# The first two blocks of a gated feed-forward layer walk the same weight chunks one step apart

## The chip, the cores and the metric

One core of a Trainium2 chip. The metric is the device time of one launch in microseconds (us). The kernel before takes 1696.36 us (median of 3 runs, 1696.3 to 1697.64).

## The reference

Pooled attention, then two feed-forward layers, all in float32:

```python
# attention: batch 8, heads 8, S 576, D 64; keys and values are means over 8 rows, 72 are left
scores = scale * q @ k_p.T; attn = softmax(scores); x = attn @ v_p     # x: 4608 tokens x 512
# layer 1 (512 -> 2048 -> 512)
h = x @ w_in
g = where(h >= 1, h, where(h <= -1, 0, (h + 1)**2 / 4))
x = g @ w_out
# layer 2 (512 -> 2048 -> 512)
out = (max(x @ w_in2, 0)**2) @ w_out2
```

The weights arrive as 64-bit floats, so that the kernel itself converts them to 32 bits.

## The kernel before

**Tiles.** 4608 tokens are 36 tiles of 128 for the attention, and 9 blocks of 512 (four tiles each) for layer 1. The 2048 hidden columns are cut in 16 chunks of 128 (`KF`). Every float32 product is made of three products in a reduced format: an operand `a` is split into `hi` (a rounded copy, written by ScalarE) and `lo` (`a - hi`, by VectorE), and `hi*hi + hi*lo + lo*hi` is summed. So a *first product* of one block and one chunk (`gemm1`, L613) is 12 matmuls of 512 columns into one bank, and a *second product* (`gemm2`, L672) is 12 into the four accumulator banks of its block.

**Steps.** The main loop (L852) goes through 144 steps of layer 1, block after block, chunk after chunk, and then 16 of layer 2's first block. Step s issues the first product of s and the second product of step s - 2 (`LAG`). `step_ops` (L627) issues what VectorE and ScalarE do for it: two activations and one VectorE instruction that make `g` from the bank (L643 to L653), `gh` and `gl`, its split (L654, L660), the split of the next weight chunks (`split_hi`, `split_lo`, L211 to L219), and, at a block's last chunk, the copy of the accumulators to DRAM (`evac_acc`).

**Weights of layer 1.** Each of the 32 chunks (16 of `w_in`, 16 of `w_out`) is loaded as 512 KB and converted once (`convert_w`, L136): two ScalarE instructions (its "head"), three VectorE instructions and one on GpSimd (its "tail"). The result stays in SBUF for all nine blocks. Its split into `hi` and `lo` does not stay: every block makes it again, for both weights. In the first block the `lo` of `w_in` is made by GpSimd from chunk 2 on (L602), later by VectorE. Conversions run through the opening and the steps of block 0.

**Attention.** It is cut in units: `k` (keys of a batch), `q` (transpose of a tile's queries), `s` (scores, half a tile each), `x` (times the values). The string `before` (L479) lists what runs ahead of the steps: keys and values of batch 0, tiles 0 to 3 (block 0), and five conversion heads. There the normalized weights are transposed by TensorE (`p` units, L422). Later tiles write them to DRAM (`do_stores`), fetch them back (`fetch`) and transpose with VectorE (`turn`, L447). The table `slots` gives each unit of the later tiles a half step: tiles 4 to 7 (block 1) lie in steps 2 to 14, those of block 2 from step 12 on.

**Who sets the order.** The order written in the program is a priority. The framework plans each engine's queue from it ahead of the run with its own table of costs, taking the first instruction whose inputs it believes to be ready; on the chip each queue then runs strictly in that order, and waits where the belief was wrong. All DMAs are issued from one queue, SP's.

Of the kernel before, what the change touches and what calls it, by code (L numbers as in the profile page):

```python
# [20 lines left out]
LAG = 2  # L21
LEAD = 8
# [9 lines left out]
def pooled_attention_moe_moe(  # L32
# [11 lines left out]
    nc = tc.nc  # L44
# [27 lines left out]
    gp = left.enter_context(tc.tile_pool(name="gp", bufs=LAG + 2))  # L72
# [9 lines left out]
    x2t = dr.tile([DM, NT], F32, name="x2t")  # L82

# [120 lines left out]
    def stream_w2(kind, f):  # L204

        t = wq.tile([P, 2, 2, HB], F32R, tag="w", name="wt")
        n = 2 * (f // NG)
        nc.sync.dma_start(out=t.bitcast(F32), in_=w2c[kind][f % NG][:, n:n + 2])
        return None, t[:, :, 0, :], t[:, :, 1, :]

    def split_hi(kind, m, f):  # L211
        src = w_sb[kind, m, f]
        hi = ws.tile(w_shape(kind), F32R, tag=f"w{kind}hi", name=f"w{kind}hi")
        lo = ws.tile(w_shape(kind), F32R, tag=f"w{kind}lo", name=f"w{kind}lo")
        nc.scalar.activation(out=hi, in_=src, func=AF.Copy)  # L215
        return src, hi, lo

    def split_lo(eng, src, hi, lo):
        eng.tensor_tensor(out=lo, in0=src, in1=hi.bitcast(F32), op=ALU.subtract)  # L219
# [122 lines left out]
    def unit_s(t, g):  # L342
# [8 lines left out]
        if g == 0:  # L351
            pn_t[t] = (
                early_pn(t) if t in (0, 1, 3) else at.tile([P, H, SP], F32, tag="pn", name="pn", bufs=1),
                at.tile([P, H, 1], F32, tag="mx", name="mx"),
            )
            if t in ON_ACT:
                sums[t] = at.tile([P, H, 1], F32, tag="sm", name="sm", bufs=3)
# [33 lines left out]
    def early_pn(t):  # L391
        flat = pad[t % 3].rearrange("p n h c -> p (n h c)")
        return flat[:, 0:H * SP].rearrange("p (h s) -> p h s", h=H)

    def norm(t):
        pn, mx = pn_t[t] if t < TB0 else pn_t.pop(t)
# [8 lines left out]
        if t < TB0:  # L405
            nc.vector.tensor_tensor(out=pn, in0=pn, in1=sm.to_broadcast([P, H, SP]), op=ALU.mult)
            return
# [43 lines left out]
    def unit_x(t):  # L451
# [30 lines left out]
        " lo hi1 lo head head"  # L482
    ).split()
    slots, pool_at = {}, {}
    for t in range(TB0, NTILE):

        if t < 2 * TB0:
            c = (2, 5, 8, 10)[t - TB0]
            at_s0, at_s1, at_q, at_x = 2 * c, 2 * c + 1, 2 * c + 2, (15, 19, 25, 29)[t - TB0]
        else:  # L490
            c = KF - 4 + 4 * (t - 2 * TB0)
            at_s0, at_s1, at_q, at_x = 2 * c, 2 * c + 2, 2 * c + 4, 2 * c + 11
        todo = {at_s0: ("s", t, 0), at_s1: ("s", t, 1), at_x: ("x", t)}
        if t + 1 < NTILE:
            todo[at_q] = ("q", t + 1)
        if t in first_tile:
            b = first_tile.index(t)
            todo.update({2 * c - 2 + i // 2: ("k", b, i) for i in (0, 2)})
            for i in range(2 * NP):
                at_p = 2 * (c + i - 8) + (i >= NP) * 8 if b > 1 else (0, 1, 2, 3, 6, 8, 10, 12)[i]  # L500
                pool_at[at_p] = 2 * NP * b + i + 1
        assert not slots.keys() & todo.keys()
        slots.update(todo)

        assert 2 * KF * (t // TB0 - 2) <= at_x - 2 < at_x + 2 < 2 * KF * (t // TB0), t
# [46 lines left out]

    def do_later():
        for f in later:
            f()
        later.clear()
# [12 lines left out]
    def do_norms():  # L569
        for t in norms:  # L570
            norm(t)
        stores.extend(norms)
        norms.clear()
# [10 lines left out]
    steps = [(0, j, f) for j in range(NB) for f in range(KF)] + [(1, 0, f) for f in range(KF)]  # L584
    NS, NS0 = len(steps), NB * KF
    split = {}
    n_split = {"i": 0, "o": 0}
    x2_t, g_t, acc = {}, {}, {}

    def next_hi(kind, n):  # L590
        s = n_split[kind]
        if s >= min(n, NS):
            return
        m, _, f = steps[s]
        split[kind, s] = split_hi(kind, m, f) if m == 0 else stream_w2(kind, f)
        n_split[kind] += 1
        return s

    def next_lo(kind, s):
        if s is None or steps[s][0] == 1:  # L600
            return
        split_lo(nc.gpsimd if kind == "i" and 2 <= s < KF else nc.vector, *split[kind, s])  # L602
# [10 lines left out]
    def gemm1(s):  # L613
        m, j, f = steps[s]
        _, wh, wl = split.pop(("i", s))
        xh, xl = x_t[j] if m == 0 else x2_t[j]
        ph = ps_h.tile([P, TB], F32, tag="h", name="ph")
        i = 0
        for kk in range(KD):
            for a, c in ((wh, xh), (wh, xl), (wl, xh)):  # L620
                if m == 1:
                    a = a.rearrange("p o (k c) -> p o k c", k=2)[:, kk // 2]
                nc.tensor.matmul(out=ph, lhsT=a[:, kk % a.shape[1], :], rhs=c[:, kk, :], start=(i == 0), stop=(i == 3 * KD - 1))  # L623
                i += 1
        return ph

    def step_ops(s, ph, evac_a, evac_b, fill):  # L627


        m, j, f = steps[min(s, NS - 1)]  # L630
        do_later()
        do_fetches()
        next_lo("o", next_hi("o", s - LAG + 2))
        if ph is not None:
            gh = gp.tile([P, TB], F32R, tag="gh", name="gh")
            gl = gp.tile([P, TB], F32R, tag="gl", name="gl")
            g = ap.tile([P, TB], F32, tag="g", name="g", bufs=1)
            u = ap.tile([P, TB], F32, tag="u", name="u", bufs=1)
            g_t[s] = (gh, gl)
            act = nc.scalar.activation  # L640
# [7 lines left out]
        next_lo("i", next_hi("i", s + 3))  # L648
        if evac_a:
            evac_a()  # L650
        if ph is not None:
# [5 lines left out]
        if fill:  # L657
            fill()
        if ph is not None:
# [7 lines left out]
        if s >= LAG:  # L667
            evac_acc(s - LAG)
# [3 lines left out]
    def gemm2(s):  # L672
        m, j, f = steps[s]
        _, wh, wl = split.pop(("o", s))
        gh, gl = g_t.pop(s)
# [13 lines left out]
    def evac_acc(s):  # L689
        m, j, f = steps[s]  # L690
# [133 lines left out]
    lo = []  # L824
    for u in before:
        op, args = u.rstrip("0123456789,"), [int(i) for i in u.lstrip(ascii_lowercase).split(",") if i]
        if op == "kv":
            pool_to(*args)
        elif op == "norm":
            norm(*args)  # L830
        elif op == "head":
            convert_head(1)
        elif op == "tail":
            convert_tail()
        elif op == "e":
            do_later()
        elif op == "hi":
            lo.append(next_hi("i", 2))
        elif op == "lo":
            next_lo("i", lo.pop(0))  # L840
        else:
            early.append(len(early))
            unit((op, *args))()
# [6 lines left out]
    first_w2, wq = 2 * KF - 4, None  # L850
    done_w2 = 0
    for s in range(NS + LAG):  # L852
        m, j, f = steps[min(s, NS - 1)]
# [3 lines left out]
        ph = gemm1(s) if s < NS else None  # L857
        evac_a = unit_at(2 * s)
        if s >= LAG:
            gemm2(s - LAG)  # L860
# [3 lines left out]
        first = s < KF and (n_conv < 2 * KF or half_done)  # L864
        step_ops(s, ph, evac_a, evac_b, (lambda: convert_tail(1)) if first else None)
# [235 lines left out]
```

## Time and profile before

| | |
|---|---|
| median of 3 runs | 1696.36 us |
| profiled execution | 1693.02 us, its span 1691.2 us |
| TensorE busy | 1615.0 us, 95% |
| VectorE busy | 1270.4 us, 75% |
| ScalarE busy | 898.2 us, 53% |
| GpSimd busy | 386.8 us, 23% |
| first matmul of a first product | 36.17 us after the span's start |
| first matmul of step 14 | 167.19 us |
| first matmul of block 2 (step 32) | 279.15 us |

Times are us from the span's start unless marked ns. PE is TensorE, PEld its weight loads, DVE VectorE, ACT ScalarE, POOL GpSimd; L219 is line 219 of the kernel. Matmuls overlap, so that the mean of one is longer than the distance between two.

### The profile page before, as it was taken

The page shows a single profiled execution, that of the slowest core. Times are in us where ns is not written, and L with a number is a line of the kernel's source. Part 1 is how long each engine was busy: PE and PEld are TensorE (multiplying, and loading weights), DVE is VectorE, ACT ScalarE, POOL GpSimd, SP SyncE. Part 2 cuts the span into 40 slices and gives each one's busy share as a digit, 9 for nine tenths or more (in the row PEclk, how much of TensorE's full clock was granted, in tenths as well). Part 3 has the DMA queues.
Part 4 walks back from the last instruction along what each step waited for, and adds up shares of the span by engine and source line. Part 5 has one row for each costly group of instructions (what it writes and reads, how often), then busy time and mean ns, then how long its engine had stood idle before and what let it go on. Part 6 is the DMA issues. An engine that isn't in the chain of part 4 may idle for free.

```text
span 1691.2 us, 23205 instructions
## 1 busy us (share of the span) xinstructions
PE 1615.0 (95%) x7720; PEld 1319.4 (78%) x7720; DVE 1270.4 (75%) x1985; ACT 898.2 (53%) x1629; POOL 386.8 (23%) x353
## 2 busy tenths in 40 slices
PE   6877999999899999999999999999999999999998
PEld 4655787878688787778788888888888888887886
DVE  7999778888878888888786462459667955884585
ACT  6655556656566565666566542336434533553353
POOL 4766235254522436232321000000000000000000
PEclk9987999999999999999999999999999999999999
DMA  9455325445435455444445076467787777777675
GB/s 239 142 172 144 105 80 157 151 128 157 127 109 170 121 157 153 138 129 124 144 170 178 7 243 216 149 194 221 199 255 217 207 196 252 217 206 224 194 206 136
DMA packets 276727, 284.69 MB, mean 168 GB/s; under 512 B 151168, under 2 KB 179840, under 8 KB 276608
## 3 DMA queue, kind: packets, MB, share of 16 engines
q1 hardware_dynamic: 276608, 283.21, 56.2%
q8 instruction: 62, 1.02, 0.2%
q14 instruction: 57, 0.47, 0.1%
HBM read 218.10 MB, written 65.01 MB: 167 GB/s over the span
## 4 chain that ended last, share of the span: by engine, by line
PE 50%; DVE 4%; DMA 2%; ACT 1%; POOL 1%; issue 1%; SPq 1%; DVEq 0%; POOLq 0%; ACTq 0%
PE dp L959 10%; PE cp L950 9%; PE acc L684 8%; PE ph L623 8%; PE dq L959 5%; PE cr L950 5%; PE dr L959 3%; PE cq L950 2%; DMA w<-w2i 1%; DVE wilo L219 1%; POOL z L160 1%; SPq L1016 0%; DMA st<-in_moe_w_out_dram 0%; DVE aT L447 0%; DMA kv<-in_v_dram 0%
## 5 line engine op out<-in xcount | busy, mean ns | idle before, releaser
L623 PE MATMUL ph<-xhi,wihi 128*128 128x512 f32 x576 | 234.1, 407 | 17.9 <-DVE g L653 17.0
L684 PE MATMUL acc<-gh,wohi 128*128 128x512 f32 x576 | 233.4, 405 | 0.0
L684 PE MATMUL acc<-gh,wolo 128*128 128x512 f32 x576 | 227.3, 395 | 3.6 <-DVE wolo L219 3.6
L623 PE MATMUL ph<-xlo,wihi 128*128 128x512 f32 x576 | 229.4, 398 | 0.8 <-DVE xlo L470 0.8
L623 PE MATMUL ph<-xhi,wilo 128*128 128x512 f32 x576 | 229.3, 398 | 0.0
L684 PE MATMUL acc<-gl,wohi 128*128 128x512 f32 x576 | 227.0, 394 | 0.0
L907 ACT ACTIVATE gh<-g 128x512 fp32r<-128x512 f32 x224 | 139.7, 630 | 151.7 <-DVE g L976 47.9
L714 DVE TENSOR_TENSOR gl<-g,gh 128x512 fp32r<-128x512 f32 x224 | 151.1, 686 | 47.7 <-ACT gh L907 46.2
L950 PE MATMUL cp<-x,w 128*128 128x512 f32 x768 | 186.5, 390 | 0.2
L293 POOL TENSOR_TENSOR kv<-kv 72x512 f32<-72x512 f32 x112 | 132.4, 1183 | 231.7 <-DMA kv<-in_v_dram 124.1
L660 DVE TENSOR_TENSOR gl<-g,gh 128x512 fp32r<-128x512 f32 x160 | 134.8, 843 | 52.2 <-ACT gh L654 49.7
L950 PEld LDWEIGHTS cp<-x,w 128*128 128x128 f32 x768 | 143.8, 188 | 31.7 <-ACT s L972 1.4
L959 PE MATMUL dp<-gh,w 128*128 128x512 f32 x512 | 161.5, 389 | 0.0
L654 ACT ACTIVATE gh<-g 128x512 fp32r<-128x512 f32 x144 | 90.5, 628 | 118.8 <-DVE g L653 118.3
L623 PEld LDWEIGHTS ph<-xhi,wihi 128*128 128x128 f32 x576 | 111.0, 193 | 48.6 <-DVE g L653 20.0
L219 DVE TENSOR_TENSOR wilo<-wi,wihi 128x512 fp32r<-128x512 f32 x130 | 101.6, 782 | 40.7 <-ACT wihi L215 39.6
L219 DVE TENSOR_TENSOR wolo<-wo,wohi 128x512 fp32r<-128x512 f32 x144 | 122.9, 853 | 10.6 <-ACT wohi L215 10.3
L623 PEld LDWEIGHTS ph<-xhi,wilo 128*128 128x128 f32 x576 | 110.9, 193 | 24.0
L684 PEld LDWEIGHTS acc<-gh,wolo 128*128 128x128 f32 x576 | 109.3, 190 | 26.0 <-DVE wolo L219 5.3
L623 PEld LDWEIGHTS ph<-xlo,wihi 128*128 128x128 f32 x576 | 111.1, 193 | 23.2 <-DVE xlo L470 1.2
L684 PEld LDWEIGHTS acc<-gl,wohi 128*128 128x128 f32 x576 | 109.4, 190 | 23.5
L684 PEld LDWEIGHTS acc<-gh,wohi 128*128 128x128 f32 x576 | 109.4, 190 | 22.1 <-issue 1.4
(138 smaller groups left out, 3082.0 us busy)
## 6 DMA issues: line engine op xcount, KB each, us to landing
w<-w2i SPq DMA_DIRECT2D x224, 256.0 KB
w<-w2o SPq DMA_DIRECT2D x224, 256.0 KB
w2i<-cb SPq DMA_DIRECT2D x32, 512.0 KB
w2o<-cb SPq DMA_DIRECT2D x32, 512.0 KB
st<-in_moe_w_out_dram SPq DMA_DIRECT2D x31, 512.0 KB
st<-in_moe_w_in_dram SPq DMA_DIRECT2D x29, 512.0 KB
pd<-pad SPq DMA_DIRECT2D x32, 384.0 KB
z<-pd SPq DMA_DIRECT2D x96, 128.0 KB
```

Source lines behind the costliest of these rows:

```text
L160: nc.gpsimd.tensor_tensor(out=z.bitcast(I32), in0=low3, in1=z.bitcast(I32), op=ALU.add)
L219: eng.tensor_tensor(out=lo, in0=src, in1=hi.bitcast(F32), op=ALU.subtract)
L293: nc.gpsimd.tensor_tensor(out=a[:, :, 0:w], in0=a[:, :, 0:w], in1=a[:, :, w:2 * w], op=ALU.add)
L623: nc.tensor.matmul(out=ph, lhsT=a[:, kk % a.shape[1], :], rhs=c[:, kk, :], start=(i == 0), stop=(i == 3 * KD - 1))
L654: act(out=gh, in_=g, func=AF.Copy)
L660: nc.vector.tensor_tensor(out=gl, in0=g, in1=gh.bitcast(F32), op=ALU.subtract)
L684: nc.tensor.matmul(out=o, lhsT=lhsT, rhs=rhs, start=(f == 0 and x == 0), stop=(f == KF - 1 and x == 2),)
L714: tt(out=out, in0=a, in1=b, op=ALU.subtract)
L907: act(out=hi, in_=a, func=AF.Copy)
L950: nc.tensor.matmul(out=out[0], lhsT=w[:, a, k, :], rhs=xq[b, i][c][:, k, :], start=(n == 0 and i in (1, 2, 7)), stop=(n == 5), skip_group_ ...
L959: nc.tensor.matmul(out=out[d], lhsT=w[:, a, d, :], rhs=x[c], start=(g == 0 and n == 0 and i in (1, 2, 7, 4)), stop=(g == NG - 1 and n == 2 ...
```

## The change

Blocks 0 and 1 go through the 16 chunks together. Step f issues the first product of block 0 with chunk f, the second product of block 0 with chunk f - 2, and the first product of block 1 with chunk f - 1 (`LB` = 1). The two first products use the same split tile of `w_in`, which therefore has three buffers; its `lo` is always made by VectorE. Block 1's `g` is not split there: it is written to DRAM (`g1`, 256 KB per chunk). From step 17 to step 25 (`START`) the second products of block 1 follow, two a step; for these `g` is loaded back (512 KB for two chunks) and split, and `w_out` is split a second time. From step 25 on everything is as before, seven steps earlier in the count. The attention of tiles 4 to 7 moves into the string `before`, in the form of the first tiles (`p` units on TensorE; nothing of it through DRAM), with batch 1's keys and values and three more conversion heads. Tiles 8 to 11 lie in steps 12 to 23.

```diff
-    gp = left.enter_context(tc.tile_pool(name="gp", bufs=LAG + 2))
+    gp = left.enter_context(tc.tile_pool(name="gp", bufs=LAG + 1))
+    g1 = [dr.tile([P, 2, TB], F32, name=f"g1{f}") for f in range(NG)]
...
+    def split_w(kind, f):
+        src = halves(w_sb[kind, 0, f])
+        t = ws.tile([P, 2, DM], F32R, tag=f"w{kind}", name=f"w{kind}hl", bufs=LB + 2 if kind == "i" else 2)
+        nc.scalar.activation(out=t[:, 0, :], in_=src, func=AF.Copy)
+        yield t
+        nc.vector.tensor_tensor(out=t[:, 1, :], in0=src, in1=t[:, 0, :].bitcast(F32), op=ALU.subtract)
+        yield
...
-        " lo hi1 lo head head"
-    ).split()
+        " lo hi1 lo head head k1,0 k1,2 s4,0 s4,1 e q5 kv14 s5,0 tail s5,1 e norm4 q6 kv16 head p4,0 p4,1 norm5 s6,0 s6,1 e tail"
+        " q7 x4 p5,0 p5,1 s7,0 norm6 s7,1 e x5 p6,0 p6,1 norm7 head x6 tail p7,0 p7,1 x7 q8 head"
+    )
+    START = KF + LB + KF // 2
...
+    plan = [([], []) for _ in range(START + (NB - 1) * KF + LAG)]
+    for f in range(KF):
+        plan[f][0].insert(0, (0, 0, f))
+        plan[f + LB][0].append((0, 1, f))
+        plan[f + LAG][1].append((0, 0, f))
+    for f in range(KF):
+        plan[KF + LAG - (f == 0) + (f + 1) // 2 - (f > 0)][1].append((0, 1, f))
...
+    def load_g():
+        if g_loads:
+            f = g_loads.pop(0)
+            t = cv.tile([P, 2, TB], F32, tag="st", name="gi")
+            nc.sync.dma_start(out=t, in_=g1[f])
+            g_in[2 * f], g_in[2 * f + 1] = t[:, 0, :], t[:, 1, :]
+
+    def split_g1(s):
+        while g_uses and g_uses[0][0] <= s:
+            u = g_uses.pop(0)[1]
+            gh = gp.tile([P, TB], F32R, tag="gh", name="gh")
+            gl = gp.tile([P, TB], F32R, tag="gl", name="gl")
+            g = g_in.pop(u[2])
+            nc.scalar.activation(out=gh, in_=g, func=AF.Copy)
+            nc.vector.tensor_tensor(out=gl, in0=g, in1=gh.bitcast(F32), op=ALU.subtract)
+            g_t[u] = gh, gl
...
+        if (m, j) == (0, 1):
+            ph = ps_a.tile([P, TB], F32, tag="a", name="ph")
...
     def step_ops(...):
-        next_lo("o", next_hi("o", s - LAG + 2))
+        if s >= KF:
+            load_g()
+        split_o(s + 1)
+        split_rest()
+        split_g1(s + 1)
...
+            if (m, j) == (0, 1):
+                if n:
+                    u = ap.tile([P, TB], F32, tag="u", name="u", bufs=1)
+                    act(out=u, in_=ph, func=AF.Relu, bias=1.0)
+                    act(out=u, in_=u, func=AF.Square, scale=0.5)
+                g = ap.tile([P, TB], F32, tag="o", name="g", bufs=4)
+                nc.vector.scalar_tensor_tensor(out=g, in0=ph, scalar=1.0, in1=u, op0=ALU.max, op1=ALU.min)
+                nc.sync.dma_start(out=g1[f // 2][:, f % 2], in_=g)
+                continue
...
-        ph = gemm1(s) if s < NS else None
+        phs = [(u, gemm1(u)) for u in first_g[:1]]
         evac_a = unit_at(2 * s)
-        if s >= LAG:
-            gemm2(s - LAG)
+        for u in second_g:
+            gemm2(u)
+        phs += [(u, gemm1(u)) for u in first_g[1:]]
         evac_b = unit_at(2 * s + 1)
```

## Rows read from the trace of the kernel before

**Rows 1.** The page, part 1: busy time (share of the span) xinstructions.
```profile
PE 1615.0 (95%) x7720; PEld 1319.4 (78%) x7720; DVE 1270.4 (75%) x1985; ACT 898.2 (53%) x1629; POOL 386.8 (23%) x353
```
**Rows 2.** Windows: opening, steps 0-13, to step 32, to layer 2; length, busy, clock, DMA.
```profile
0.00:36.17 36.17, 19.43 (x153) 15.99 (x153) 27.38 (x48) 22.41 (x68) 16.52 (x26) 1.00 0.97 235
36.17:167.19 131.02, 103.48 (x568) 82.40 (x569) 128.12 (x178) 79.22 (x147) 90.73 (x70) 0.86 0.54 160
167.19:279.15 111.96, 110.60 (x562) 89.98 (x560) 90.03 (x139) 62.91 (x116) 41.43 (x41) 1.00 0.34 93
279.15:978.50 699.35, 677.52 (x3344) 550.52 (x3345) 558.58 (x889) 428.83 (x791) 238.10 (x218) 0.99 0.44 137
```
**Rows 3.** PE in order of time: start, us; two steps apart, and around 133.
```profile
298.66 0.39 PE L623 MATMUL ph<-xhi,wihi 128*128 128x512 f32 x1
304.10 0.39 PE L623 MATMUL ph<-xhi,wihi 128*128 128x512 f32 x1
...
132.95 1.98 PE L457 MATMUL px<-aT,vp 72*64 72x128 f32 x16 [7.62 <-DVE aT L447]
```
**Rows 4.** Groups on DVE, 36 to 168 (busy, mean ns).
```profile
L660 DVE TENSOR_TENSOR gl<-g,gh 128x512 fp32r<-128x512 f32 x14 | 14.1, 1008 | 0.0
L219 DVE TENSOR_TENSOR wolo<-wo,wohi 128x512 fp32r<-128x512 f32 x13 | 12.8, 983 | 0.1
L410 DVE TENSOR_TENSOR pad<-pn,sm 128x256 f32<-128x256 f32 (+1 forms) x12 | 10.3, 893 | 0.0
L653 DVE SCALAR_TENSOR_TENSOR g<-ph,u 128x512 f32<-128x512 f32 x14 | 9.5, 678 | 0.2 <-ACT u L644 0.2
L363 DVE TENSOR_REDUCE mx<-pss 128x4 f32<-128x288 f32 x10 | 4.5, 450 | 1.9 <-PE pss L347 1.9
L370 DVE TENSOR_TENSOR pn<-pss,mx 128x288 f32<-128x288 f32 x10 | 4.5, 447 | 0.0
L447 DVE STREAM_TRANSPOSE aT<-z 96x1024 f32<-96x1024 f32 x3 | 3.7, 1231 | 0.0
L401 DVE TENSOR_REDUCE sm<-pn 128x8 f32<-128x576 f32 x4 | 3.0, 743 | 0.0
L470 DVE TENSOR_TENSOR xlo<-px,xhi 128x512 fp32r<-128x512 f32 x4 | 2.7, 680 | 0.0
L403 DVE TENSOR_SCALAR sm<-sm 128x8 f32<-128x8 f32 x4 | 2.0, 500 | 0.0
```
**Rows 5.** The line L219: ns min/median/max, first and last start.
```profile
L219 DVE TENSOR_TENSOR wolo<-wo,wohi x144: 674/685/1840, 43.8 to 979.6; 128x512 fp32r<-128x512 f32 x144
```
**Rows 6.** Groups on DVE in the opening, 0 to 36.
```profile
L406 DVE TENSOR_TENSOR pn<-pn,sm 128x576 f32<-128x576 f32 x1 | 0.7, 745 | 0.0
L403 DVE TENSOR_SCALAR sm<-sm 128x8 f32<-128x8 f32 x4 | 0.6, 160 | 0.0
L404 DVE RECIPROCAL sm<-sm 128x8 f32<-128x8 f32 x4 | 0.8, 193 | 0.0
L288 DVE TENSOR_REDUCE kp<-kv 72x128 f32<-72x1024 f32 x4 | 7.3, 1873 | 5.3 <-DMA kv<-in_k_dram 5.3
```
**Rows 7.** Groups on POOL, 36 to 168.
```profile
L219 POOL TENSOR_TENSOR wilo<-wi,wihi 128x512 fp32r<-128x512 f32 x14 | 21.2, 1517 | 4.5 <-PE pq L331 3.2 <-issue 1.3
L293 POOL TENSOR_TENSOR kv<-kv 72x512 f32<-72x512 f32 x9 | 13.2, 1471 | 0.0
L293 POOL TENSOR_TENSOR kv<-kv 72x256 f32<-72x256 f32 x9 | 9.2, 1027 | 0.5
```
**Rows 8.** Groups on PE, 36 to 168: the attention.
```profile
L347 PE MATMUL pss<-kbd,qT 128*128 128x144 f32 (+1 forms) x48 | 9.0, 341 | 1.9 <-DVE pn L370 1.5 <-ACT kbd L314 0.4
L457 PE MATMUL px<-aT,vp 72*64 72x64 f32 (+1 forms) x64 | 5.5, 332 | 17.1 <-DVE aT L447 14.6 <-POOL vp L294 2.5
L304 PE MATMUL pk<-ident,kv 72*64 72x72 f32 x128 | 4.8, 228 | 0.0
L331 PE MATMUL pq<-ident,q 128*128 128x128 f32 x16 | 2.9, 312 | 5.3 <-issue 5.3
```
**Rows 9.** Groups on PE in the opening: the transposes of the p units.
```profile
L422 PE MATMUL pt<-ident,pad 128*72 128x128 f32 x24 | 3.3, 274 | 0.8 <-DVE pad L406 0.8
```
**Rows 10.** Groups on ACT, 36 to 168.
```profile
L215 ACT ACTIVATE wohi<-wo 128x512 fp32r<-128x512 f32 x14 | 8.8, 625 | 2.8 <-PE acc L684 2.3 <-POOL wo L160 0.5
L654 ACT ACTIVATE gh<-g 128x512 fp32r<-128x512 f32 x14 | 8.8, 630 | 16.5 <-DVE g L653 16.3
```

More of the change, by code (lines that the diff above doesn't have):

```diff
@@ L21 @@
 LAG = 2
+LB = 1
 LEAD = 8
@@ L571, in do_norms @@
             norm(t)
-        stores.extend(norms)
+        stores.extend(t for t in norms if t >= 2 * TB0)
         norms.clear()
@@ new lines, in pooled_attention_moe_moe @@
+    for f in range(KF):
[4 more added lines that the diff above has]
+        plan[KF + LAG - (f == 0) + (f + 1) // 2 - (f > 0)][1].append((0, 1, f))
+    rest = [(0, j, f) for j in range(2, NB) for f in range(KF)] + [(1, 0, f) for f in range(KF)]
+    for n, u in enumerate(rest):
+        plan[START + n][0].append(u)
+        plan[START + n + LAG][1].append(u)
+    NS0 = START + (NB - 2) * KF
@@ new lines, in pooled_attention_moe_moe, with split_rest, split_start @@
+    NS = NS0 + KF
+    i_uses = [(n, u) for n, p in enumerate(plan) for u in p[0] if u[:2] != (0, 1)]
+    o_uses = [(n, u) for n, p in enumerate(plan) for u in p[1]]
+    g_uses = [(n, u) for n, u in o_uses if u[:2] == (0, 1)]
+    g_loads = list(range(NG))
+    wi_t, wo_t, g_in = {}, {}, {}
+    x2_t, g_t, acc = {}, {}, {}
+    half_split = []
+    def split_rest():
+        for c in half_split:
+            next(c)
+        half_split.clear()
+    def split_start(kind, f):
+        c = split_w(kind, f)
+        half_split.append(c)
+        return next(c)
@@ L666, in step_ops, with gemm2 @@
         do_later()
-        if s >= LAG:
-            evac_acc(s - LAG)
+        for u in plan[s][1]:
+            evac_acc(u)
         if evac_b:
             evac_b()
[L672 to L675, printed above, removed]
+    def gemm2(u):
+        m, j, f = u
+        w = wo_t.pop(u)
+        wh, wl = (w[:, :, n, :] if m else w[:, n, :] for n in range(2))
+        gh, gl = g_t.pop(u)
         if f == 0:
@@ L687, in gemm2, with evac_acc @@
                 )
-    def evac_acc(s):
-        m, j, f = steps[s]
+    def evac_acc(u):
+        m, j, f = u
         if f < KF - 1:
@@ L823, in pooled_attention_moe_moe @@
         nc.gpsimd.memset(t, 0.0)
[L824 to L843, printed above, removed]
+    do_now(before)
     norms.clear()
@@ L849, in pooled_attention_moe_moe @@
     n_w2 = NG * 2 * 9
-    first_w2, wq = 2 * KF - 4, None
+    first_w2, wq = START + 2, None
     done_w2 = 0
-    for s in range(NS + LAG):
-        m, j, f = steps[min(s, NS - 1)]
+    for s, (first_g, second_g) in enumerate(plan):
+        m, j, f = first_g[-1] if first_g else (1, 0, KF - 1)
         if s == max(slots) // 2 + 3:
```

132 lines of the change are left out of this document (70 added, 62 removed), and 1 row of the table before.

## The prediction

> **What bounds the kernel now.** I read the page's busy times first, then windows by stage, then the groups of the stage that is worst. On the whole span TensorE is 95% busy [rows 1], so what can be won lies where it is not. The windows show the place [rows 2]: in steps 0 to 13 (131.0 us) TensorE is busy 103.5, at a granted clock of 0.86, while VectorE is busy 128.1 of 131.0. The next 18 steps run at TensorE's pace: 110.6 of 112.0, VectorE at 90.0. The stage of steps 32 to 143 loses 21.8 in 699, and the opening is short of loads: its DMA share is 0.97 at 235 GB/s. So only the steps in which weights are converted are VectorE's, and there TensorE has about 27 us idle and works part of the rest at the lower clock.
>
> The undisturbed pace is 5.44 us for two products (304.10 - 298.66) [rows 3], 2.72 each. Queues are strict: at 132.95 TensorE stood 7.62 us before units of the attention although products stood behind them [rows 3].
>
> **The change, part by part.** I compare the start of block 2. Before it is 279.15, with two second products still open; after it (step 25) one is open, so the old point to compare with is 279.15 + 2.72 = 281.9.
>
> *VectorE until the end of step 13.* It has 128.1 now [rows 2].
> - 14 `lo` splits of `w_in` come over from GpSimd. The like instruction for `w_out` takes 0.685 as median of the whole run and 0.983 in this stage [rows 4, 5]: 9.6 to 13.8. I take 0.85, between them, as GpSimd will be quieter: +11.9.
> - 13 `g` of block 1 at 0.678 [rows 4]: +8.8.
> - The attention of tiles 4 to 7 leaves in its old form. The seven groups of it are 10.3 + 4.5 + 4.5 + 3.7 + 3.0 + 2.7 + 2.0 [rows 4]: -30.7. It comes back in the form of the opening: per tile two maxima 0.90, two subtractions 0.89, the sum 0.74, small ones 0.35, the weighting 0.745, the `lo` of x 0.68 [rows 4, 6], 4.3 in all: +17.2. Tile 8 in steps 12 and 13: scores 1.8, sum and small ones 1.1, three pieces of padding at 0.86 [rows 4]: +5.5.
> - GpSimd loses 21.2 of its 90.7 us [rows 2, 7]. Instructions that it can hold up are the 128.1 less `g`, maxima, subtractions, transposes, sums and x (27.9), 100.2; `wolo` is longer by (983 - 685)/983 = 30% here [rows 4, 5], so about 30 us of these 100 are waiting, and 21.2/90.7 of that goes: -7.1 (bounds 0 and -21.2).
>
> Together +5.6: 133.7, and with the 2.9 that it waits now, 136.6.
>
> [...]
>
> *TensorE until the end of step 13.* 14 first and 12 second products as now, 26 x 2.72 = 70.7; 13 more first products, 35.4; the attention of the stage, 9.0 + 5.5 + 4.8 + 2.9 = 22.2 [rows 8]; 32 transposes of weights that the opening's form needs: 24 took 3.3 [rows 9], so 4.4. Sum 132.7 at full clock.
>
> Both engines thus need 133 to 137 us where they now need 128 and about 93. Without any overlap of the added products it would be 136.6 + 35.4 = 172; with all of it 136.6. I take 145: near the lower end, since VectorE lost only 2.9 of 131.0 to waiting [rows 2], but with 8.4 us more, for the cover is gone; TensorE had 27 us to spare and has 4.
>
> *Other queues in that stage.* ScalarE is busy 79.2 of 131.0 [rows 2]; 13 pairs of activations for block 1 add about 16, less its share of the attention: hidden. SP gets 16 stores of 256 KB and 8 loads of 512 KB, 8.4 MB in over 200 us, some 40 GB/s beside 160 and 93 where the opening carries 235 [rows 2]: hidden; the loads wait behind the fetches of tiles 9 to 11, which I put into the stalls below. Batch 1's keys and values and tiles 5 to 8's queries are moved ahead in the same queue, past weight loads; the opening has no DMA left over, so it is this that I expect to stretch.
>
> *Steps 14 to 24.* 5 first and 19 second products remain, 24 x 2.72 = 65.3. The attention of tiles 8 to 11: between steps 14 and 32 now four tiles cost 112.0 - 36 x 2.72 = 14.1 with 1.4 idle [rows 2]; I take 12 of these, as part of tile 8 is done. VectorE has 4 instructions a step and is no bound there. Stalls: block 1's first second product needs the accumulators that block 0's last one has just left, with no first product between, 0 to 2.7, I take 1. In the paired steps `w_out` has two buffers, and the second split of a step waits for the step before to be done; if `gh` and `gl` stand behind it in the queues, each pair pays 0.625 + 0.630 for ScalarE and 0.685 to 1.0 for VectorE [rows 4, 5, 10], 2.2; if not, nothing. Eight pairs: 0 to 18; the planner may place ready work ahead, so I take 4.
>
> *Later.* Layer 2's weight preparation goes over 106 steps where it had 112; of the 21.8 us lost in that stage [rows 2] perhaps 5% more: +1.
>
> **The sum.** 36.2 + 145 + 65.3 + 12 + 5 = 263.5 against 281.9: -18.4, +1 later, -17.4. The profiled execution took 1693.02, so 1675.6 as such; the median of the runs stands 3.3 above it, so 1679.0.
>
> **The rivals.**
> - *The opening does not overlap (slower).* Batch 1's chain (loads, four poolings of values on GpSimd, tile 4's x) is strict, and TensorE's first product may stand behind tile 7's units. The second four tiles then cost what the first four do without the wait for keys, 36.2 - 5.3 [rows 2, 6], and 4.8 for the pooling of keys [rows 8]: the steps begin at 71.9. If the 14 steps then still take 131.0, the end is 71.9 + 131 + 82.3 = 285.2, and with the later 1 the time is 1700.7. It loses from a beginning at 67.6 on. For it: the loads at 235 GB/s, and 14.6 us of TensorE before units of the attention [rows 8]. Against: the 14 steps have then lost the attention of tiles 4 to 7, and the planner can place products of block 0 between.
> - *The pairs are bound by the chain over two buffers (no change).* All eight pay 2.2: 17.6 + 1 where I have 5, so 1692.6. Against: the attention's units fill part of it.
> - *TensorE is the bound all the way (faster still).* 133 for the stage and no stall in the pairs: 1679 - 12 - 5 = 1662. For it: the lower clock of 0.86 [rows 2] comes with idle time, which goes.
>
> **How the numbers follow.** A measurement of this kernel can tell about 0.2% from no change, 3.4 us. Forecast 0.50, with a range of its own of 1666 (stage 137, no stall in the pairs) to 1690 (stage 153, 8 in the pairs); slower rival 0.21; pairs 0.12; TensorE-bound 0.12; the rest for what I do not see. The range takes in the third rival and the first with a little above: 1660 to 1704. Faster by over 0.2%: the forecast, the third rival and half of the second, 0.67; within: half of the second and a part of the first, 0.12; slower 0.21.
>
> **What would show it.** Right: the first matmul of block 2 near 264; in the steps before, TensorE and VectorE both over 90% busy and the granted clock nearer 1; `wilo` on VectorE near 0.85; the paired steps about 6 us each. Wrong: the steps begin late with both engines idle; gaps of 2 us before every pair, ended by `gl`; TensorE waiting in steps 17 to 21 for a load of `g`; or a stage of steps 32 to 143 (now 25 to 136) that has grown by more than a few us.

## The result, and the profile after

The changed kernel takes 1704.30 us, median of 6 runs (1700.80 to 1707.53), against 1695.92 (1693.75 to 1697.64, 6 runs) for the kernel before: a ratio of 1.0051, 95% interval 1.0037 to 1.0065. It is 8.4 us slower where 17.4 faster was forecast, and just above the range that the prediction gave (1660 to 1704). The profiled execution took 1705.93, 12.9 more than that of before; 4.5 of these 12.9 are the scatter of single executions.

One correction to the diff quoted above: the new line of the order reads `lo hi1 lo head k1,0 ...`, with one `head` there and not two. The opening thus has seven conversion heads, two more than the five of before.

Page of the changed kernel, part 1, which answers to [rows 1]: busy time, share of the span, instructions.

```profile
PE 1625.3 (95%) x7752; PEld 1327.5 (78%) x7752; DVE 1254.0 (74%) x1971; ACT 887.8 (52%) x1621; POOL 361.9 (21%) x339
```

The engines as a whole tell little: VectorE has 16 us less work and TensorE 10 more, and their shares hardly move. The stages do. Windows of the changed kernel, to be held against [rows 2]: stretch, length, busy time of PE, PEld, DVE, ACT and POOL with instructions, granted clock, DMA share, GB/s. The first row is the opening, the second the part of it behind the point where the old kernel began its products; then steps 0 to 13, steps 14 to 24, and block 2 to layer 2.

```profile
0.00:75.69 75.69, 48.67 (x449) 40.30 (x449) 59.26 (x106) 43.84 (x110) 37.18 (x47) 0.81 0.72 186
36.04:75.69 39.65, 27.44 (x297) 22.65 (x293) 31.61 (x61) 22.67 (x46) 22.06 (x24) 0.69 0.52 143
75.69:197.57 121.88, 113.39 (x482) 90.61 (x481) 104.64 (x144) 78.86 (x139) 62.09 (x52) 0.98 0.51 155
197.57:281.60 84.03, 77.56 (x398) 62.76 (x396) 59.41 (x99) 38.54 (x73) 16.14 (x18) 0.96 0.46 130
281.60:992.10 710.50, 681.86 (x3336) 553.39 (x3335) 564.19 (x889) 422.17 (x790) 246.53 (x224) 0.98 0.45 135
```

The reader is to see two things. The second row holds 39.65 us in which no product of block 0 or 1 runs, at a granted clock of 0.69, a mean between the two levels of 1.2 and 2.4 GHz. The first matmul of a first product is the one at its end (start, length, engine, line):

```profile
75.69 0.80 PE L696 MATMUL ph<-xhi,wihl 128*128 128x512 f32 x1
```

And the last row, whose program the change hardly touches, is 11 us longer than its counterpart, though one second product less is open at its start. Hardly, since the preparation of layer 2's weights began four steps ahead of block 2 before and begins two steps behind it now: all 16 groups of that preparation lie in the last row, where one of them was done ahead of it before, and GpSimd has 224 instructions there instead of 218.

| us | first product | first of block 2 | first of layer 2 | block 2 to layer 2 |
|---|---|---|---|---|
| before | 36.2 | 279.2 | 978.7 | 699.6 |
| before, less one second product (2.72) | | 281.9 | | 696.9 |
| forecast | 36.2 | 263.5 | 961.4 | 697.9 |
| after | 75.7 | 281.6 | 992.1 | 710.5 |

So in these traces the change gains 0.3 us until block 2 where 18.4 was forecast, and loses 13.6 behind it where 1 was forecast. They are one execution of each kernel; in which stage the 4.5 us of scatter lie can't be told from them, and all lengths of stages below carry an uncertainty of that size. Layer 2 takes the same in both kernels within half a microsecond.

### The profile page after: what moved, and what is told of

Read it like the earlier page. It is cut to its first block, busy times and chain, and to the rows that moved or that the text cites. A ratio compares the mean times of both kernels' runs of the same rounds, so it can differ in the third digit from the quotient of the medians.

```text
span 1704.1 us, 23203 instructions
## 1 busy us (share of the span) xinstructions
PE 1625.3 (95%) x7752; PEld 1327.5 (78%) x7752; DVE 1254.0 (74%) x1971; ACT 887.8 (52%) x1621; POOL 361.9 (21%) x339
## 4 chain that ended last, share of the span: by engine, by line
PE 60%; DVE 16%; DMA 6%; ACT 5%; POOL 4%; issue 4%; SPq 4%; DVEq 0%; POOLq 0%; ACTq 0%
PE ph L696 12%; PE acc L773 11%; PE dp L1030 10%; PE cp L1021 10%; PE dq L1030 5%; PE cr L1021 5%; SPq L254 3%; PE dr L1030 3%; PE cq L1021 2%; DVE wohl L221 2%; DMA st<-in_moe_w_in_dram 2%; DVE gl L748 2%; POOL z L164 2%; DVE wihl L221 1%; DMA st<-in_moe_w_out_dram 1%
## 5 line engine op out<-in xcount | busy, mean ns | idle before, releaser
L696 PE MATMUL ph<-xhi,wihl 128*128 128x512 f32 x1152 | 389.5, 401 | 16.1 <-DVE g L741 7.6
L773 PE MATMUL acc<-gh,wohl 128*128 128x512 f32 x1152 | 366.9, 399 | 12.4 <-ACT gh L669 5.6
L696 PEld LDWEIGHTS ph<-xhi,wihl 128*128 128x128 f32 x1152 | 221.1, 192 | 72.5 <-DVE g L741 10.0
L773 PEld LDWEIGHTS acc<-gh,wohl 128*128 128x128 f32 x1152 | 213.8, 190 | 59.3 <-DVE wohl L221 6.2
L696 PE MATMUL ph<-xlo,wihl 128*128 128x512 f32 x576 | 229.1, 398 | 0.0
L773 PE MATMUL acc<-gl,wohl 128*128 128x512 f32 x576 | 226.4, 393 | 0.0
L221 DVE TENSOR_TENSOR wihl<-wi,wihl 128x512 fp32r<-128x512 f32 x128 | 110.2, 861 | 45.6 <-ACT wihl L219 45.5
L221 DVE TENSOR_TENSOR wohl<-wo,wohl 128x512 fp32r<-128x512 f32 x144 | 121.6, 845 | 11.2 <-ACT wohl L219 11.0
L696 PEld LDWEIGHTS ph<-xlo,wihl 128*128 128x128 f32 x576 | 110.9, 192 | 22.3 <-issue 0.3
L773 PEld LDWEIGHTS acc<-gl,wohl 128*128 128x128 f32 x576 | 108.9, 189 | 23.5 <-DVE gl L670 0.2
```

The costliest lines, as they stand in the source:

```text
L221: nc.vector.tensor_tensor(out=t[:, 1, :], in0=src, in1=t[:, 0, :].bitcast(F32), op=ALU.subtract)
L696: nc.tensor.matmul(out=ph, lhsT=a, rhs=c[:, kk, :], start=(i == 0), stop=(i == 3 * KD - 1))
L773: nc.tensor.matmul(out=o, lhsT=lhsT, rhs=rhs, start=(f == 0 and x == 0), stop=(f == KF - 1 and x == 2),)
```

## Experiments on the opening

The theory was that the new order of the opening costs its whole length, since it is written as one strict string with all the attention of tiles 4 to 7 ahead of the first product. The rival: VectorE has that work to do wherever it stands, so the place does not matter.

**The opening alone.** The kernel before with the new string of the opening; block 1 is not joined and the weights are prepared as before.

```diff
-        " lo hi1 lo head head"
+        " lo hi1 lo head k1,0 k1,2 s4,0 ... x7 q8 head"
-    for t in range(TB0, NTILE):        # attention planned into the steps
+    for t in range(2 * TB0, NTILE):
```

> The kernel before with one part of the change: tiles 4 to 7 of the attention in the opening, as the changed kernel has them; weights, products and steps as before, nothing shared. Theory 'the opening does not overlap': the changed kernel's opening takes 39.7 us more in which no product runs, and 14 steps without that attention still need about 103 us of VectorE (128.1 - 30.7 + 5.5), so block 2 starts near 289 (before: 279.2), and the time is 1700 to 1712. Rival 'the opening costs little by itself, the sharing is what takes long': block 2 within 4 us of 279 and a time of 1692 to 1700.

Measured: 1699.53 us, ratio 1.0036 (1.0024 to 1.0049). The first product starts at 75.7, block 2 at 303.3: 24.2 later than before, more than the 10 expected. The rival falls by that start; the time, though, lies half a microsecond below the theory's range and inside the rival's, because the stage behind block 2 got shorter (the second row). Windows of this kernel, opening's end to block 2 and block 2 to layer 2:

```profile
75.70:303.30 227.60, 196.13 (x865) 154.71 (x863) 200.72 (x262) 133.03 (x245) 125.70 (x108) 0.95 0.42 130
303.30:985.70 682.40, 672.69 (x3348) 547.27 (x3347) 543.99 (x873) 421.88 (x774) 214.88 (x199) 1.00 0.42 130
```

The attention taken out of the steps gives back 15.4 of the 39.5 us that the opening takes (243.0 us from first product to block 2 before, 227.6 here). The rest of the change, the sharing of weights above all, then brings block 2 from 303.3 to 281.6, 24.4 us like for like, that is with one second product open in both (303.3 + 2.7 - 281.6). The two cancel. The second row is a surprise that the next section is about: the program of block 2 to layer 2, whose code is unchanged, is 17 us *shorter* here than before. A part of its work had run ahead: the first prepared weights of layer 2 (`cb`) are written at 179.5, where before it is 251.4, and GpSimd has 199 instructions in the stage instead of 218 (214.88 us against 238.10 [rows 2]).

**The same attention beside products.** The changed kernel, with the units of tiles 4 to 7 cut out of the string and issued after the second products of steps 0 to 4; block 1 joins from slice 4 on, and makes up slices 0 to 3 at the end (a slice is a chunk). The string ends in three conversion heads instead; with it three tails leave the opening for the steps, so it is not the attention alone that moves.

```diff
+    parts = ["k1,0 k1,2 s4,0 ... norm4", "s5,0 ... norm5", "s6,0 ...", "s7,0 ...", "x6 ... q8"]
+        if s < len(parts):
+            do_now(parts[s])
-        plan[f + LB][0].append((0, 1, f))
+        plan[f + LB if f >= JOIN else KF + LB + f][0].append((0, 1, f))
```

> The changed kernel with the attention of tiles 4 to 7 spread over steps 0 to 4, beside block 0's products, instead of in the opening. Block 1 joins at step 5 with chunk 4; its chunks 0 to 3 follow in steps 17 to 20 with their weights split once more (4 splits, some 3 us of VectorE). All else is as changed. Theory 'the opening does not overlap': block 2 starts near 263 (257 to 270) where the changed kernel has 281.6, and the time is 1680 to 1692. Rival 'VectorE is the bound in any order': block 2 not before 275, and a time of 1697 or more.

Measured: 1712.92, ratio 1.0114 (1.0096 to 1.0133). The first product starts at 36.6 and block 2 at 273.6: 8.0 earlier than in the changed kernel and 8.3 better than before like for like, but short of the 257 to 270 expected; it beats the rival's 275 by 1.4. So of the 18.1 us that block 2 came late against the forecast (281.6 - 263.5), 8.0 came back with the opening's order, and the other 10 did not. The time is in the rival's range, as the stage behind has grown again, to 722.9 us. The windows of this kernel:

```profile
36.60:273.60 237.00, 212.43 (x1161) 168.14 (x1161) 204.24 (x302) 137.37 (x256) 102.65 (x92) 0.96 0.51 150
273.60:996.50 722.90, 683.42 (x3348) 554.75 (x3347) 564.28 (x892) 422.64 (x793) 247.89 (x224) 0.97 0.44 133
```

## Experiments on the stage that the change does not touch

What TensorE waits for in that stage: engine, tile and line, who ends the wait, us in all, times, longest. First the kernel before, from 279 to 978:

```profile
PE ph L623 <- DVE g L653: 13.8, 7, 5.4
PE px L457 <- DVE aT L447: 3.7, 2, 2.2
PE acc L684 <- DVE wolo L219: 3.6, 4, 1.4
PE pss L347 <- ACT kbd L314: 1.4, 1, 1.4
```

Then the changed one, from 282 to 992:

```profile
PE px L460 <- DVE aT L450: 15.1, 5, 4.9
PE ph L696 <- DVE g L741: 7.6, 5, 3.6
PE acc L773 <- DVE wohl L221: 4.2, 4, 1.6
PE acc L773 <- ACT wohl L219: 1.2, 1, 1.2
PE acc L773 <- DVE o L787: 0.5, 1, 0.5
```

The waits before products (`ph`) shrink, and those of the attention's last unit (`px`, the weighted values) for its transpose (`aT`) grow from two to five and from 3.7 to 15.1 us. In all TensorE is idle 28.6 us where it was 21.8. These 6.8 us are half of the 13.6; the other half is TensorE's own busy time, 681.9 us against 677.5 with one second product more, at a granted clock of 0.98 against 0.99 [rows 2]. One of the `px` waits, in order of time (start, length, engine, line; in brackets the wait before it). GpSimd, ScalarE, VectorE, TensorE:

```profile
619.47 1.73 POOL L296 TENSOR_TENSOR kv<-kv 72x512 f32<-72x512 f32 x1
...
624.56 0.74 POOL L201 TENSOR_TENSOR z<-z,s 128x256 f32<-128x256 f32 x1
```
```profile
622.38 0.63 ACT L174 ACTIVATE cb<-s 128x512 fp32r<-128x512 f32 x1 [2.30 <-POOL s L199]
...
625.33 0.63 ACT L174 ACTIVATE cb<-z 128x512 fp32r<-128x512 f32 x1 [2.32 <-POOL z L201]
...
626.34 0.62 ACT L219 ACTIVATE wihl<-wi 128x512 fp32r<-128x512 f32 x1
```
```profile
626.99 1.31 DVE L221 TENSOR_TENSOR wihl<-wi,wihl 128x512 fp32r<-128x512 f32 x1 [3.24 <-ACT wihl L219]
...
628.83 1.23 DVE L450 STREAM_TRANSPOSE aT<-z 96x1024 f32<-96x1024 f32 x1
```
```profile
630.20 1.98 PE L460 MATMUL px<-aT,vp 72*64 72x128 f32 x16 [4.46 <-DVE aT L450]
```

ScalarE stands twice, 2.30 and 2.32 us, at a conversion of layer 2's weights (`cb`) for sums that GpSimd makes between poolings of keys and values. The split of the step's own weights (`wihl`) is queued behind it, VectorE stands 3.24 for that, and the transpose is behind VectorE's split. TensorE then meets `px` with its products queued behind it. Over the stage none of these three engines is near its limit (VectorE 564 of 710 us busy); four strict queues pass one delay on.

**Is it the preparation of layer 2's weights?** Both kernels with it left out: zeros are stored in its place, so layer 2 multiplies zeros.

```diff
     def prepare_w2(kind, g):
+        for n in range(9):
+            if n % 2 == 0 and n < 8:
+                ...   # memset on GpSimd, one store
+            yield
```

> The changed kernel without the work of layer 2's weight preparation: no load, conversion, split or sum of these weights; GpSimd writes zeros into a tile and SP stores it in the places where the prepared parts would go (layer 2 then multiplies by zeros; its time is not looked at). What is looked at is the stage from block 2 to layer 2, 710.5 in the changed kernel, beside the same cut in the kernel before (699.6 whole). Theory 'the preparation's instructions in the queues of ScalarE and VectorE make the stalls': the stage falls to 672 to 688 in both and they lie within 5 us of each other. Rival 'the new steps place the attention's x units too early by themselves': the changed kernel's stage stays 10 us or more above the other's, with px waiting for aT.

> The kernel before with the same cut: no work of layer 2's weight preparation, zeros stored in its place. Theory 'the preparation's instructions make the stalls': the stage from block 2 to layer 2 falls from 699.6 to 672 to 688, as in the changed kernel with the cut. Rival 'the new steps by themselves': this one falls, the changed kernel's doesn't by as much.

Measured: changed kernel 1659.09 (ratio to before 0.9790, 0.9775 to 0.9806), kernel before 1666.16 (0.9832, 0.9817 to 0.9847). The stage, first row the changed kernel, second the kernel before, both under the 672 to 688 expected and within 5 of each other as expected:

```profile
282.60:947.50 664.90, 664.90 (x3335) 544.50 (x3334) 448.36 (x761) 359.32 (x662) 147.90 (x158) 1.00 0.38 119
```
```profile
283.30:951.40 668.10, 668.10 (x3348) 546.64 (x3347) 458.17 (x765) 371.18 (x665) 147.67 (x152) 1.00 0.37 116
```

TensorE is busy all the time at the full clock in both, and the stages differ by 3.2 us, the one open product and half a microsecond. So the loss behind block 2 comes with the preparation: it costs 31.5 us of the stage in the kernel before (699.6 - 668.1) and 45.6 in the changed one (710.5 - 664.9). Under the same cut the changed kernel is 7.1 us the faster one (medians of 4 runs). In the two traces 3.9 of that stand until layer 2 (947.5 against 951.4), and 3.1 in layer 2 itself (711.0 against 714.1), which neither kernel changes; so the gain of the sharing is rather 4 us than 7. And the cut moves the order ahead of block 2 too: in the kernel before that block starts at 283.3 with it, 279.2 without.

**Is it too dense?** It goes over 106 steps instead of 112. Theory: spread over more steps in the changed kernel it costs less, and over fewer in the old one more.

```diff
# changed kernel
-    first_w2, wq = START + 2, None
+    first_w2, wq = START - 4, None
# kernel before
-    first_w2, wq = 2 * KF - 4, None
+    first_w2, wq = 2 * KF + 2, None
```

> The changed kernel with layer 2's weight preparation begun at step 21, four before block 2, so that its 144 pieces lie over 112 steps as in the kernel before, where the changed kernel has 106. Theory 'the denser preparation makes the later stage longer': from block 2's start to layer 2's first product it goes from 710.5 back to 697 to 701, the time to 1690 to 1697. Rival 'the planner's order over the whole later stage came out worse, the density is not it': that stage stays over 704, and the time is 1699 to 1709.

> The kernel before with layer 2's weight preparation begun at step 34, two after block 2's start, so that its 144 pieces lie over 106 steps as in the changed kernel. Theory 'the denser preparation makes the later stage longer': the stage from block 2 to layer 2 goes from 699.6 to 707 or more, the time to 1702 to 1710. Rival 'the density is not it': that stage within 4 us of 699.6, the time 1692 to 1700.

Measured: 1705.77, ratio 1.0062 (1.0047 to 1.0077), stage 715.1, of whose idle 30.6 us all stand before `px`; and 1693.12, ratio 0.9989 (0.9979 to 1.0000), stage 696.3. The theory asked for 701 or less in the first and 707 or more in the second; neither moves its way, and it falls.

**Is it the buffers?** The change takes one of four buffers from `g` and gives the split weights of `w_in` a third. In the kernel before the first was done alone and then both, and the third buffer was taken out of use for the later stage in the changed kernel and in the one of the second experiment.

```diff
# one, in the kernel before; the next has both lines
-    gp = ...(name="gp", bufs=LAG + 2)
+    gp = ...(name="gp", bufs=LAG + 1)
+    hi, lo = ws.tile(..., bufs=3 if kind == "i" else 2)
# changed kernel, and the one with the attention beside products
+        if s == START:
+            held = ws.tile([P, 2, DM], F32R, tag="wi", ...)   # written once, read at the stage's end
```

> The kernel before with three buffers instead of four for gh and gl (LAG + 1, as in the changed kernel); nothing else. So far the stage from block 2 to layer 2 took 682 to 700 us in the three kernels with the old steps and 710 to 723 in the three with the new ones, where TensorE waits for the transposed weights (px for aT). Theory 'three buffers of the split of w_in let the planner run VectorE ahead': no effect here, that stage within 690 to 702, time 1690 to 1699. Rival 'three buffers of gh and gl tie VectorE to TensorE': the stage over 706, time over 1700.

> The kernel before with three buffers for the split of w_in, hi and lo, as in the changed kernel (and three for gh and gl, which makes the room); the steps are the old ones and nothing is shared. Theory 'three buffers of the split of w_in let the planner run VectorE ahead': the stage from block 2 to layer 2 becomes 706 to 720 with waits of px for aT of 10 us or more in all, the time 1702 to 1715. Rival 'it is some other part of the new steps': stage 690 to 702, time 1690 to 1699.

> The changed kernel in which a dummy tile holds one of the three buffers of the split of w_in from block 2 on (one column copied into it at step 25, and read at the end of block 8), so that the later stage has two, as the kernel before. Theory 'three buffers of the split of w_in let the planner run VectorE ahead': the stage from block 2 to layer 2 falls from 710.5 to 685 to 702, the time to 1682 to 1697. Rival 'some other part of the new steps': the stage stays over 705, the time 1699 to 1709.

> The changed kernel with the attention of tiles 4 to 7 beside block 0's products (as in the run where block 1 joins at step 5; block 2 started there at 273.6) and a dummy tile that holds one of the three buffers of the split of w_in from block 2 on. Theory 'three buffers': the later stage falls from 722.9 to 685 to 702, the time to 1675 to 1692. Rival: stage over 710, time over 1700.

| kernel | median us | ratio (95%) | block 2 | stage |
|---|---|---|---|---|
| before, `g` with three buffers | 1694.71 | 1.0000 (0.9991 to 1.0008) | 279.5 | 703.1 |
| and a third for `w_in` | 1699.62 | 1.0024 (1.0015 to 1.0033) | 280.4 | 707.2 |
| changed, third buffer held | 1704.61 | 1.0064 (1.0051 to 1.0077) | 287.2 | 709.1 |
| beside products, third buffer held | 1714.96 | 1.0119 (1.0106 to 1.0132) | 277.7 | 724.1 |

With the third buffer held, the stage stays within 1.4 us of what it was (710.5 and 722.9). In the old kernel both together add 7.6 us to the stage, 4.1 of them beyond the buffers of `g` alone, but 1.0 of its idle time stands before `px`, not the 10 or more that the theory asked for; the waits are others. The third buffer alone is not what makes the changed kernel's loss. The third row also shows how far block 2 itself moves: 287.2 against 281.6, though the hold begins only there.

**Is it the layout?** The change puts both halves of a split weight into one tile. The changed kernel with two tiles, and the kernel before with one tile and the changed kernel's buffers:

```diff
# changed kernel
-        t = ws.tile([P, 2, DM], ...)
+        t = [ws.tile([P, DM], ...) for x in ("hi", "lo")]
# kernel before, on top of the three buffers
+        t = ws.tile([P, 2] + w_shape(kind)[1:], ...)
+        hi, lo = t[:, 0], t[:, 1]
```

> The changed kernel with hi and lo of a split weight in two tiles instead of in one (same bytes, three buffers for w_in, two for w_out), as the kernel before has them. If the planner's order of the later stage comes from that layout, the stage from block 2 to layer 2 falls from 710.5 to 702 or less, the time to 1697 or less. If the layout is nothing to it, the stage stays at 706 to 716 and the time at 1700 to 1708.

> The kernel before with the buffers of the changed one: hi and lo of a split weight in one tile, three for w_in, two for w_out, three for gh and gl; steps, opening and products as before. If the layout makes the later stage longer, the stage from block 2 to layer 2 goes from 699.6 (707.2 with three buffers in two tiles) to 710 or more, and the time to 1703 or more. If not, it is 695 to 709 and the time 1692 to 1701.

Measured: 1707.73, ratio 1.0082 (1.0069 to 1.0096), stage 715.0, with 21.4 us of `px` waits; and 1685.66, ratio 0.9953 (0.9941 to 0.9966), stage 689.4 without a `px` wait. The theory falls, the wrong way round once more; the second time lies below the range of either. This second kernel is the fastest of all that compute the result. Its stage:

```profile
281.20:970.60 689.40, 678.24 (x3348) 551.88 (x3347) 554.48 (x887) 421.03 (x790) 240.97 (x218) 0.99 0.44 136
```

It does the same work as before on every engine within 2% [rows 2]; TensorE waits 11.2 us in it, where it waited 21.8. Buffers and order differ, not the work.

**Is it the place of `px` in the queues?** If a transpose and its `px` stand too close in the queues, a later `px` has to help. So the last units of the attention were planned one step later, for tiles 12 to 35: in the changed kernel, in the kernel before, in the kernel with the attention beside products, and in the changed kernel with the load of `g` one step earlier as well (the stall of steps 17 to 24, below).

```diff
# changed kernel; in the kernel before the same shift, + 2 half steps for t >= 3 * TB0
-    at_s0 + 4, at_s0 + 11
+    at_s0 + 4, at_s0 + 13
# the last of the four besides
-        if s >= KF:
+        if s >= KF - 1:
             load_g()
```

> The changed kernel with the x units of tiles 12 to 35 one step later (half step + 13 instead of + 11); nothing else. Theory 'the queues have the turn and the x unit too close together': the waits of px for aT fall from 15.1 us to under 4, the stage from block 2 to layer 2 from 710.5 to 692 to 702, the time to 1686 to 1697. Rival 'the waits are a symptom, VectorE is late with all it does': px waits go, but others (ph for g, acc for the split of w_out) take their place, the stage stays over 705, the time over 1699.

> The kernel before with the same shift of the x units of tiles 12 to 35. There px waits for aT only 3.7 us. Theory 'turn and x unit too close in the changed kernel alone': little happens, the stage from block 2 to layer 2 stays within 6 us of 699.6, the time 1689 to 1700. If it gains 8 us or more here too, the distance is not what sets the two kernels apart.

> The changed kernel with the attention of tiles 4 to 7 beside block 0's products (block 1 joins at step 5) and the x units of tiles 12 to 35 one step later. Its block 2 started at 273.6, 8 us ahead of the changed kernel, and its later stage took 722.9 with 27 us of px waits. Theory: px waits under 5 us, stage 692 to 705, time 1680 to 1697. Rival 'symptom': stage over 712, time over 1702.

> The changed kernel with the x units of tiles 12 to 35 one step later and each load of g issued one step earlier. In the changed kernel one second product of block 1 waited 5.6 us for gh, ScalarE stood for the load of g, and that load stood behind 28 DMA issues for a tile of queries in SP's queue; 12 matmuls at the lower clock followed. Theory: that stall goes, block 2 starts at 274 to 278 instead of 281.6, and the time is 4 to 8 us under that of the shift alone. Rival 'another wait takes its place': block 2 at 280 or later, no difference between the two.

| kernel, `px` one step later | median us | ratio (95%) | block 2 | stage | `px` waits |
|---|---|---|---|---|---|
| changed | 1696.29 | 1.0007 (0.9995 to 1.0020) | 282.1 | 702.6 | 0.4 |
| before | 1709.94 | 1.0084 (1.0071 to 1.0097) | 278.6 | 716.9 | 0 |
| beside products | 1705.16 | 1.0061 (1.0044 to 1.0079) | 276.0 | 716.6 | 4.1 |
| changed, `g` loaded earlier | 1707.57 | 1.0075 (1.0062 to 1.0089) | 274.7 | 719.4 | 7.4 |

In the changed kernel the `px` waits go, 14.7 us, and with them 7.9 us of the stage and 8.0 of the time: it equals the kernel before. The rival is half right, for other waits take up 8.4 us of it (28.6 - 15.1 = 13.5 before the shift, 22.3 - 0.4 = 21.9 with it). In the kernel with the attention beside products it is right altogether: the `px` waits fall from 27.3 to 4.1 and the stage only from 722.9 to 716.6, over the 712 that it named. And the same shift in the kernel before costs 17.3 us of the stage, at other units. The largest waits of its TensorE, from 279 to 995:

```profile
PE pk L309 <- DVE xlo L470: 9.8, 3, 5.2
PE ph L623 <- DVE g L653: 9.5, 9, 2.2
PE acc L684 <- DVE wolo L219: 7.6, 5, 2.5
```

The last kernel's front is 7.4 us shorter (274.7 against 282.1), 1.7 of it ahead of the first product (75.1 against 76.8) and most of the rest from that stall, which shrinks from 5.4 to 1.2; its stage is 16.8 longer, and the time 11.3 over that of the shift alone where 4 to 8 under it was expected. So a later `px` is no rule; it is a cure for one order of the queues.

## Why the prediction was wrong, step by step

**"14 steps in 145 us" failed, and with it the sum.** From 36.2 to the first product of step 14 (197.57) it took 161.4: 39.65 of opening and 121.88 of steps. The amounts of work were about right. VectorE was put at 133.7 and did 31.61 + 104.64 = 136.3; TensorE was put at 132.7 at full clock and was busy 27.44 + 113.39 = 140.8, part of it at 0.69. What was wrong was to let them overlap. The allowance for lost cover was 8.4 us, taken from how little VectorE waits in the old steps [rows 2]; but the added work of the opening runs ahead of the first product in every queue, so nothing of 39 products stands beside it. TensorE was idle 12.2 us in the opening's second part and 8.5 in the steps. So of the 16.4 us missed some 8 are TensorE busy longer than its sum at full clock (140.8 - 132.7), and some 8 idle beyond the 12.3 that 145 left it. The largest waits in the opening's second part, as the trace of the changed kernel has them:

```profile
PE pss L350 <- ACT kbd L317: 7.8, 2, 5.4
PE pt L425 <- DVE pad L409: 2.7, 2, 1.7
```

The first is the chain of keys of batch 1, the second the weighting of a tile ahead of its transpose; the sum priced their work and not their waits. The order of the string shows them without a run: `k1`, `s4`, `p4` and `x4` follow each other, with heads and tails of weights between and no product. That the place in the string is the cause is shown by run for 8.0 us, the start of block 2 won by putting the attention beside products; for the rest it is the reading of this trace.

**VectorE's relief was right, and so was the lower price of contention.** In steps 0 to 13 VectorE is busy 104.64 of 121.88, TensorE 113.39: the bound has moved to TensorE, as the third rival had it, but behind an opening. Groups of VectorE in those steps: out<-in, shapes, count, busy us, mean ns, idle before.

```profile
L158 DVE TENSOR_SCALAR wi<-wi 128x512 uint32<-128x512 uint32 x10 | 11.1, 1111 | 0.3
L748 DVE TENSOR_TENSOR gl<-g,gh 128x512 fp32r<-128x512 f32 x14 | 11.0, 782 | 9.1 <-ACT gh L742 8.9
L221 DVE TENSOR_TENSOR wohl<-wo,wohl 128x512 fp32r<-128x512 f32 x12 | 9.8, 820 | 0.0
L741 DVE SCALAR_TENSOR_TENSOR g<-ph,u 128x512 f32<-128x512 f32 x14 | 9.6, 688 | 4.1 <-ACT u L719 4.0
L221 DVE TENSOR_TENSOR wihl<-wi,wihl 128x512 fp32r<-128x512 f32 x12 | 8.7, 728 | 0.0
L734 DVE SCALAR_TENSOR_TENSOR g<-ph,u 128x512 f32<-128x512 f32 x12 | 8.2, 681 | 0.0
```

The `lo` of `w_in` was put at 850 ns and took 728; that of `w_out` fell from 983 to 820, `gl` from 1008 to 782 [rows 4], as GpSimd went from 90.7 of 131.0 us busy [rows 2] to 62.1 of 121.9. `g`, with one input from PSUM, has 681 and 688 as it had 678. The Trainium skill, "SBUF — State Buffer", section "Who interferes with whom", says that a VectorE instruction with two SBUF inputs contends with a GpSimd instruction that reads SBUF, and that one with at most one SBUF input, outside what it calls the 2-port perf modes, does not. `gl`, `lo` and `g` agree with it. It does not free every instruction with one SBUF input: a shift of the conversions (`L158`) has one, and its mean in these steps is 1111 ns for `w_in`, where 428 is the median of the whole run; whether it ran in such a mode no run here shows. The price here lies between the bounds of the forecast: the means came down, and `w_out`'s stayed above the 685 that is its median in the whole run [rows 5].

**Steps 14 to 24 came out right, in part by luck:** 84.0 us, forecast 82.3. All that TensorE waited there:

```profile
PE acc L773 <- ACT gh L669: 5.6, 1, 5.6
PE acc L773 <- DVE o L787: 0.8, 1, 0.8
```

The paired steps did not wait for `gl` or for a buffer of `w_out`, so the second rival is out. The sum set 5 us aside for the accumulators (1) and the pairs (4); these took 0.8 and nothing, and a load of `g`, which was named among the signs but priced only as part of these stalls, took 5.6. SyncE's queue, ScalarE and TensorE:

```profile
241.34 13.13 SPq L254 DMA_DIRECT2D q<-in_q_dram  x28
254.51 0.43 SPq L660 DMA_DIRECT2D gi<-g  x1
```
```profile
258.95 1.15 ACT L669 ACTIVATE gh<-gi 128x512 fp32r<-128x512 f32 x2 [3.93 <-DMA gi<-g]
```
```profile
259.63 1.22 PE L773 MATMUL acc<-gh,wohl 128*128 128x512 f32 x2 [5.58 <-ACT gh L669]
```

The load stands behind 28 issues of queries, 13.13 us in one queue. Loading one step earlier left 1.2 us of the stall.

**"Later: +1" failed by 12.6 us.** It scaled 21.8 us of idle time by the number of steps, as if density set it; that theory fell on the chip in both directions. The loss comes with layer 2's preparation: without it neither kernel waits in the stage. Half of it shows as waits, the `px` waits above all, and half as busy time at a lower granted clock; moving `px` removes its waits and 7.9 us of the stage. What is not settled is which part of the change tips the order there: buffers, layout and density, each tried alone, did not carry it over or take it away. Much the same work took from 689 us (one tile for both halves) to 717 with the old steps, and from 703 to 724 with the new ones; 682 with the new opening alone, but with a part of the work done ahead. A forecast of a planned order at this load needs some 20 us of uncertainty for a stage that it does not touch.

**The slower rival** had the place right (steps begin at 71.9; measured 75.7) and a time, 1700.7, close to the measured 1704.3, but by other terms. It let the steps take 131 us and put block 2 at 285.2; they took 121.9 and it came at 281.6. What made the kernel slower than before is the stage that this rival left alone. Of the sum's miss, 30.7 us up to layer 2's first product in the profiled execution, 16.4 belong to the opening with steps 0 to 13, 1.7 to steps 14 to 24, and 12.6 to the later stage. The gain of 0.3 us until block 2 is itself not firm: in the runs with these steps, this opening and this load of `g` that block came between 278.2 and 287.2.

## What to carry to other kernels

Work moved ahead of a loop is paid there in full where nothing of the loop stands beside it in the order, and may give back less than that in the loop (here 15.4 of 39.5 us); so read the order in which each queue gets it, not only the busy times. Where a planner orders several strict queues, compare the untouched stages first after any change, and run both kernels without the background work: that tells the gain of the idea (here some 4 us up to layer 2) from the disturbance of the order (here 14), as far as the cut itself does not move the order. An order that has come out well is worth as much as an idea: buffers and layout alone, with no work removed, made the kernel before 0.5% faster (ratio 0.9953, 0.9941 to 0.9966).

## What the runs showed that was not expected

- Small shifts of the order that leave the work of the engines as it is moved a 700-us stage by as much as the whole gain that was sought: one step later for `px` gave -7.9 in one kernel and +17.3 in the other.
- A gain ahead of a stage can be lost in it: 7.4 us won by an earlier load came with 16.8 lost (719.4 against 702.6).
- The preparation of layer 2's weights brings no engine but TensorE near its limit, VectorE at 558.58 of 699.35 [rows 2], and still costs 31.5 us of that stage, 21.8 of it as waits of TensorE; the rest is TensorE's own busy time, 677.5 against 668.1, at a granted clock of 0.99 against 1.00. Without it TensorE waits for nothing in 668.1 us.
